# Two last steps of a token-mixing kernel change places, and the new last step gives its results in halves

## The chip, the cores and the metric

The kernel runs on one core of one Trainium2 chip. The metric is device time in microseconds, lower is better.

## What is computed

The input x has 8 batches of 4224 tokens and 192 channels. The first part of the reference is a causal 7-tap convolution along the tokens with softmax weights per head. On its result the second part mixes tokens with two 4224 x 4224 matrices, and then channels:

```python
theta = x @ w_theta
zr, zi = x * cos(theta), x * sin(theta)
y = einsum('ts,bsd->btd', w_tok_r, zr) + einsum('ts,bsd->btd', w_tok_i, zi)
u = x + y
out = u + maximum(u @ w_ch, 0)
```

Nearly all the work is in the two token products: for each of the 33 blocks of 128 output tokens, a sum over all 4224 input tokens, with 8 x 192 = 1536 columns. A 128 x 1536 result is called a row block here.

## The kernel before

**Chunks and steps.** The input tokens are cut into 33 chunks of 128. Eleven chunks are kept on the chip at a time, each as a tile `z` with seven fp16 planes: four products of x with cosine and sine, and sums and differences of them. The row blocks are taken in pairs, 17 units in all; the last unit has one block (32), since 33 is odd. The kernel goes round the units in 58 steps, t = 0 to 57. A step takes one unit and all chunks that are on the chip, multiplies them, adds the products to the unit's row block tiles `pv`, and writes these to scratch memory for the unit's next turn. A row block is finished at its unit's last turn. Towards the end fewer chunks are left for a step: step 55 has 6, step 56 (blocks 30 and 31) has 4, step 57 (block 32 alone) has 2.

**What a step does.** `load_w` (L316) fetches the two matrices' pieces into `st` by DMAs on POOL's queue, four for each matrix; there are two `st` buffers, one for each matrix, so the next step's load waits until the last transpose of the buffer. `turn` (L334) transposes a piece in 32 x 32 blocks on VectorE into a weight tile `wt`; `wsum` (L342) makes sums and differences of weight tiles, also on VectorE. For a pair of blocks, seven products per chunk do the work of eight: four transposes and four sums (S1 to S4) prepare the weights. For a single block there are two transposes, no sum, and four products. `mix` (L430) issues the products: for each entry of the list that `runs` (L410) returns, all the step's chunks in turn, two matmuls of 384 columns each (q = 0 and 1, the two halves of the columns), which accumulate in a PSUM tile `y` of two banks. Two such tiles exist. At the end of an entry, `give` (L400) has VectorE add the accumulator to one half (h) of the channels of a row block; the accumulator may go on after that.

**The end of a row block.** `cast` (L460) makes fp16 of half the row block (column group g, 768 columns), on ScalarE, or on VectorE for g = 0 in the last two steps. `turn_u` (L467) transposes it by six PE transposes (L165) into a PSUM tile `tp`, which ScalarE evacuates to `uT` (L151). `output` (L473) multiplies by `w_ch` in eight matmuls (L141) into a PSUM tile `v`; then one VectorE instruction (L476) adds the positive part to the row block, and one DMA on SP's queue (L481) writes 384 KB to the output. `tp` and `v` take turns in two PSUM buffers.

**Order.** The order on each engine is written down by hand: `pe`, `dve`, `act` and `pool` chain an engine's instructions in the order in which they are called. Within a step, `mix` calls events between products. An event's place is a number from 0 to 7, the share of the step in sevenths. The next step's transposes and sums are events of the current step (`w_tasks`, L354, called in `step_events`), and so are its loads of row blocks (`load_rows`, L365, on SP's queue), the weight loads of the step after it, and the casts, transposes and outputs of finished blocks (`outputs`, L486), which are placed by an estimate of the products' time, 0.324 us for each pair of matmuls.

Of the kernel before, what the change touches and what calls it, by code (L numbers as in the profile page):

```python
# [16 lines left out]
def kernel(  # L17
# [23 lines left out]
    nc = tc.nc  # L41
# [42 lines left out]
    def pe(ins):  # L84
        return in_order("pe", ins)

    def dve(ins):
        return in_order("dve", ins)
# [64 lines left out]
    def turned():  # L153
        return wk.tile([P, 12, P], F16, name="uT", tag="uT")
# [5 lines left out]
    def transposed(uT, u, gs, by_dve=False):  # L160

        tp = banks("tp", F16)
        for g in gs:
            for k in range(6):
                pe(nc.tensor.transpose(  # L165
                    tp[:, g, k * P : (k + 1) * P],
                    u[:, g * GC + k * P : g * GC + (k + 1) * P], ident,
                ))
        g = slice(gs[0], gs[-1] + 1)
        evacuate(  # L170
            uT[:, :, :].rearrange("p (g k) s -> p g (k s)", g=NG)[:, g, :],
            tp[:, g, 0 : 6 * P], by_dve,
        )
# [111 lines left out]
    class Step:  # L285


        def __init__(self, t):
            self.t, self.u, self.ks = t, unit(t), active(t)
            self.n = len(self.ks)  # L290
            self.tbs = [tb for tb in (2 * self.u, 2 * self.u + 1) if tb < NT]
            self.pair = len(self.tbs) == 2
            self.first = t < NU
            self.final = t + NU >= NSTEP
            self.late = self.final and self.n < NW
            visits = [v for v in range(NU, NSTEP) if v % NU == t % NU]
            quiet = [v for v in visits if start[2 * NW - 1] < v <= 2 * NU]
            self.adds, self.ahead = [], []
            for i, tb in enumerate(self.tbs):
                known = self.known(tb)  # L300
                if t not in ([v for v in quiet if known < v - 1] or visits[-1:])[:1]:
                    continue
                if not self.late:
                    self.adds.append(i)
                else:
                    far = known <= start[2 * NW - 1]
                    self.ahead.append((i, 2 * NU - NW + 2 * (t % NU) if far else start[-1],
                                       (t // NU - 1 - far) % 2))
            self.time = 0.324 * self.n * (7 if self.pair else 4)
            self.st, self.w, self.xr, self.ub, self.uT, self.pv = {}, {}, {}, {}, {}, []  # L310

        def known(self, tb):
# [41 lines left out]
        def w_tasks(self):  # L354

            if not self.pair:
                return [(0.25, lambda: self.turn("11")), (4.2, lambda: self.turn("12"))]
            return [
                (0.25, lambda: self.turn("11")), (1.2, lambda: self.turn("21")),
                (2.05, lambda: self.wsum("S3")), (2.2, lambda: self.turn("22")),  # L360
                (3.05, lambda: self.wsum("S1")), (3.3, lambda: self.wsum("S2")),
                (4.2, lambda: self.turn("12")), (5.1, lambda: self.wsum("S4")),
            ]
# [33 lines left out]
                    accum_op=ALU.add,  # L397
                ))

        def give(self, y, i, h, copies):  # L400
            o = self.pv[i][:, :].rearrange(
                "p (q b h e) -> p q b h e", q=2, h=2, e=HD
            )[:, :, :, h, :]
            yv = y[:, :, 0:BH].rearrange("p q (b e) -> p q b e", e=HD)
            if self.first and copies:
                act(nc.scalar.activation(out=o, in_=yv, func=AT.Copy))  # L406
            else:
                dve(nc.vector.tensor_tensor(out=o, in0=yv, in1=o, op=ALU.add))  # L408

        def runs(self):  # L410


            if self.pair:
                return [
                    ("11", Z11, "c1", True, (0, 0, True)),
                    ("S1", T1, "c2", True, (1, 1, True)),
                    ("S2", T2, "c1", False, (0, 1, True)),
                    ("S4", Z22, "c2", False, (0, 1, False)),
                    ("S3", T3, "c1", False, (1, 1, False)),
                    ("12", Z21, "c3", True, (0, 0, False)),  # L420
                    ("22", T4, "c1", False, (1, 0, True)),
                ]
            return [
                ("11", Z11, "c1", True, (0, 1, True)),
                ("11", T1, "c2", True, None),
                ("12", Z21, "c1", False, (0, 0, True)),
                ("12", Z22, "c2", False, (0, 1, False)),
            ]

        def mix(self, events):  # L430

            runs = self.runs()
            events = sorted(events, key=lambda e: e[0])
            y = {}
            for r, (wn, zn, cn, opens, to) in enumerate(runs):
                if opens:
                    y[cn] = ypool.tile([P, 2, PC], F32, name="y", tag="y")
                for c, k in enumerate(self.ks):
                    while events and events[0][0] * len(runs) <= 7 * (r + c / self.n):
                        events.pop(0)[1]()  # L440
                    yield k
                    for q in range(2):
                        pe(nc.tensor.matmul(  # L443
                            y[cn][:, q, 0:BH],
                            lhsT=self.w[wn][:, c, :, :].rearrange("p bt i -> p (bt i)"),
                            rhs=chunks[k].z[:, zn, q * BH : (q + 1) * BH],
                            start=(opens and c == 0), stop=(c == self.n - 1),
                            skip_group_check=True,
                        ))
                if to:  # L450
                    self.give(y[cn], *to)
            for _, f in events:
                f()
            if not self.final:
                for i, tb in enumerate(self.tbs):
                    nc.sync.dma_start(
                        out=part[(self.t // NU) % 2][tb, :, :], in_=self.pv[i]
                    )

        def cast(self, i, g):  # L460
            if g == 0:
                self.ub[i] = wk.tile([P, N], F16, name="ub", tag="ub", bufs=2)
                self.uT[i] = turned()
            cols = slice(g * GC, (g + 1) * GC)
            evacuate(self.ub[i][:, cols], self.pv[i][:, cols], self.t >= NSTEP - 2 and g == 0)

        def turn_u(self, i, g):  # L467
            transposed(self.uT[i], self.ub[i], [g])

        def cross_u(self, i):  # L470
            crossed(self.uT[i], self.ub[i])

        def output(self, i, g):  # L473
            u = self.pv[i][:, g * GC : (g + 1) * GC]
            ub = u.rearrange("p (k n) -> p k n", k=2)
            dve(nc.vector.scalar_tensor_tensor(  # L476
                out=ub, in0=channel_mix(self.uT[i][:, 6 * g : 6 * g + 6, :], wch), scalar=0.0, in1=ub,
                op0=ALU.max, op1=ALU.add,
            ))
            rows = slice(self.tbs[i] * P, (self.tbs[i] + 1) * P)  # L480
            nc.sync.dma_start(  # L481
                out=out[g * GB : (g + 1) * GB, rows, :].rearrange("b s d -> s b d"),
                in_=u.rearrange("p (b d) -> p b d", d=D),
            )

        def outputs(self):  # L486

            found = []
            for i in range(len(self.tbs)):
                if not self.late:  # L490
                    at = 1 if i or not self.pair else 0.9 - self.time / 7
                    for g in range(NG):
                        found.append((at + g, lambda i=i, g=g: self.cast(i, g)))
                        found.append((12 + 5.5 * i + 2.7 * g,
                                      lambda i=i, g=g: self.output(i, g)))
                    found.append((at + 2, lambda i=i: self.cross_u(i)))
                    continue
                at = 1.2 if i or not self.pair else 0.6 - self.time / 7
                every, turn, mix = 2.0, 1.2, 3.6
                for g in range(NG):  # L500
                    found.append((at, lambda i=i, g=g: self.cast(i, g)))
                    found.append((at + turn, lambda i=i, g=g: self.turn_u(i, g)))
                    found.append((at + mix, lambda i=i, g=g: self.output(i, g)))
                    at += every
            return found

    steps = [Step(t) for t in range(NSTEP)]
    outputs = [
        (sum(s.time for s in steps[: t + 1]) + at, f)
        for t in range(NSTEP) if steps[t].final for at, f in steps[t].outputs()  # L510
# [233 lines left out]
```

## Time and profile before

| | |
|---|---|
| median of three runs | 1448.68 us (1447.93 to 1449.42) |
| span of the profiled execution, first to last instruction | 1444.6 us |
| mean granted clock of TensorE | 0.997 |
| PE busy | 1414.5 us, 98% of the span |
| VectorE (DVE) busy | 978.2 us, 68% |
| ScalarE (ACT) busy | 316.2 us, 22% |
| start of the last product of L443 | 1429.4 us |
| end of the last instruction of VectorE | 1440.2 us |

The page gives the profiled execution by its span; a time of its own is not listed for it, and the median of the runs lies 4.1 us above the span. In rows of the order in time, the columns are the start, the duration (both us), the engine, the line, the operation, the tiles written and read with their shapes, the number of merged instructions, and in brackets the idle time before it and who ended it. PE's rows for matmuls include some 0.16 us of pipeline after the last issue, so that neighbouring rows overlap. In the table by stretches the numbers after the window are its length, then the busy time and count of PE, PEld (weight loads), DVE, ACT and POOL, the granted clock, the share of the DMA engines and GB/s.

### The profile page before, as it was taken

Reading aid. Unit: us, or ns where it says so; the run is one execution under the profiler, and the core shown is the slowest. Engines: PE = TensorE matmul, PEld = TensorE weight load, DVE = VectorE, ACT = ScalarE, POOL = GpSimd, SP = SyncE. Lnnn points to the kernel's source line nnn. Section 1 sums busy time; section 2 is a strip of 40 time slices with the busy share of each in tenths; the row PEclk is TensorE's granted clock in tenths of the full one; section 3 lists DMA queues with packets and bytes.
Section 4 is the critical chain, followed back from the end, with each engine's and each line's share of the span. In section 5 each row is a group of like instructions: output and inputs, shape, how many; then the busy total and the mean of one; then the engine's idle time right before and its main releaser. Section 6 shows DMA issues by size and latency. Waiting matters only on the chain.

```text
span 1444.6 us, 23749 instructions
## 1 busy us (share of the span) xinstructions
PE 1414.5 (98%) x9809; PEld 886.3 (61%) x9809; DVE 978.2 (68%) x1050; ACT 316.2 (22%) x379; POOL 434.6 (30%) x655
## 2 busy tenths in 40 slices
PE   7899999999999999999999999999999999999997
PEld 4656666666666666666666666666666666666665
DVE  6893554555448687866666657876877677767686
ACT  6851101111124254000000004435210110010133
POOL 8421211111223232432433343233323123213120
PEclk9999999999999999999999999999999999999999
DMA  9975756564699999897899889989999999898883
GB/s 181 253 148 136 146 119 133 98 152 87 152 229 210 226 244 222 219 265 173 223 245 222 233 155 239 235 181 237 274 220 202 213 204 221 204 200 193 166 232 116
DMA packets 272029, 281.99 MB, mean 195 GB/s; under 512 B 106672, under 2 KB 240176, under 8 KB 271920
## 3 DMA queue, kind: packets, MB, share of 16 engines
q0 software_dynamic: 162464, 92.15, 48.4%
q1 hardware_dynamic: 71824, 178.88, 35.2%
q10 hardware_dynamic: 37632, 9.44, 4.3%
q8 instruction: 77, 1.26, 0.4%
q14 instruction: 32, 0.26, 0.1%
HBM read 245.49 MB, written 108.13 MB: 245 GB/s over the span
## 4 chain that ended last, share of the span: by engine, by line
PE 89%; DVE 3%; DMA 2%; ACT 2%; POOL 1%; issue 1%; SPq 0%; DVEq 0%; ACTq 0%; POOLq 0%
PE y L443 81%; PE v L141 5%; PE pc L210 1%; PE tp L165 1%; ACT z L246 1%; DVE pv L408 1%; DMA xw<-xw 1%; POOL xw L197 1%; DMA xw<-in_x_dram 1%; DVE z L257 1%; POOL st L323 1%; DVE z L251 1%; DMA pv<-part 1%; ACT uT L151 1%; DVE wt L336 0%
## 5 line engine op out<-in xcount | busy, mean ns | idle before, releaser
L443 PE MATMUL y<-z,wt 128*128 128x384 f16 x7656 | 1283.6, 326 | 10.4 <-DVE pv L408 7.3
L443 PEld LDWEIGHTS <-wt 128*128 128x128 f16 x7656 | 740.7, 98 | 488.1 <-issue 10.2
L408 DVE TENSOR_TENSOR pv<-y,pv 128x768 f32<-128x768 f32 x324 | 309.2, 955 | 327.0 <-PE y L443 286.8
L336 DVE STREAM_TRANSPOSE wt<-st 128x1408 f16<-128x1408 f16 (+7 forms) x224 | 327.8, 1465 | 45.8 <-PE y L443 39.1
L323 POOL DMA_DIRECT2D st<-in_moe_w_tok_r_dram x232 | 132.4, 579 | 464.9 <-DVE wt L336 459.4
L323 POOL DMA_DIRECT2D st<-in_moe_w_tok_i_dram x232 | 132.5, 580 | 405.4 <-DVE wt L336 397.5
L348 DVE TENSOR_TENSOR wt<-wt 128x1408 f16<-128x1408 f16 (+7 forms) x216 | 176.1, 815 | 40.5 <-PE y L443 38.0
L151 ACT ACTIVATE z<-pc 128x768 f16<-128x768 f32 x65 | 53.3, 820 | 386.7 <-PE pc L210 386.5
L151 ACT ACTIVATE ub<-pv 128x768 f16<-128x768 f32 x63 | 50.2, 835 | 333.2 <-DVE pv L408 310.7
L406 ACT ACTIVATE pv<-y 128x768 f32<-128x768 f32 x66 | 54.0, 819 | 281.6 <-PE y L443 281.6
L141 PEld LDWEIGHTS <-uT 128*128 128x128 f16 x1056 | 91.1, 98 | 27.4 <-issue 8.5
L386 POOL TENSOR_TENSOR pv<-pv,xr 128x1536 f32<-128x1536 f32 x24 | 74.5, 3105 | 67.1 <-DVE pv L476 21.9
L197 POOL DMA_DIRECT2D xw<-in_x_dram x132 | 76.5, 591 | 30.1 <-DMA xw<-xw 9.7
L476 DVE SCALAR_TENSOR_TENSOR pv<-v,pv 128x768 f32<-128x768 f32 x66 | 62.9, 954 | 27.5 <-PE v L141 27.0
L151 ACT ACTIVATE uT<-tp 128x1536 f16<-128x1536 f16 (+1 forms) x49 | 59.7, 1221 | 74.4 <-PE tp L165 74.4
L257 DVE TENSOR_TENSOR z<-z 128x768 f16<-128x768 f16 x132 | 73.4, 556 | 3.6
L246 ACT ACTIVATE z<-v,half_pi 128x768 f16<-128x768 f32 x66 | 59.9, 907 | 42.1 <-PE v L141 41.7
L251 DVE TENSOR_TENSOR z<-z 128x1536 f16<-128x1536 f16 x66 | 60.1, 948 | 6.6 <-ACT z L246 6.6
L141 PE MATMUL v<-wth,uT 128*128 128x192 f16 x528 | 55.0, 248 | 5.6 <-ACT z L246 3.3
L141 PE MATMUL v<-wch,uT 128*128 128x192 f16 x528 | 54.2, 246 | 2.1 <-DVE pv L476 1.2
L246 ACT ACTIVATE z<-v 128x768 f16<-128x768 f32 x66 | 53.5, 810 | 0.0
L210 PE MATMUL pc<-xw,bands 96*64 96x192 f16 x528 | 35.3, 256 | 1.2 <-DVE bands L628 0.8
(43 smaller groups left out, 138.0 us busy)
## 6 DMA issues: line engine op xcount, KB each, us to landing
part<-pv SPq DMA_DIRECT2D x79, 768.0 KB, 4.6
pv<-part SPq DMA_DIRECT2D x79, 768.0 KB, 6.0
out_dram<-pv SPq DMA_DIRECT2D x66, 384.0 KB, 4.3
st<-in_moe_w_tok_r_dram POOLq DMA_DIRECT2D x136, 176.0 KB, 5.7
st<-in_moe_w_tok_i_dram POOLq DMA_DIRECT2D x136, 176.0 KB, 5.1
xs<-z SPq DMA_DIRECT2D x132, 96.0 KB, 4.1
xw<-in_x_dram POOLq DMA_DIRECT2D x121, 96.0 KB, 5.9
xr<-xs SPq DMA_DIRECT2D x24, 384.0 KB, 4.5
```

The costliest lines, as they stand in the source:

```text
L141: pe(nc.tensor.matmul(v[:, k, b * D : (b + 1) * D], lhsT=tT[:, 3 * k + b + i, :], rhs=w[:, 2 * b + i, :], start=(i == 0), stop=(i == 1),))
L151: act(nc.scalar.activation(out=out, in_=in_, func=AT.Copy))
L197: nc.gpsimd.dma_start(out=self.xw[lo : lo + n, h, :, :], in_=x[:, t0 : t0 + n, :].rearrange("b s d -> s b d"),)
L246: act(nc.scalar.activation(**args))
L251: dve(nc.vector.tensor_tensor(out=o, in0=xv, in1=o, op=ALU.mult))
L257: dve(nc.vector.tensor_tensor(out=z[:, o, :], in0=z[:, a, :], in1=z[:, b, :], op=ALU.subtract))
L323: pool(nc.gpsimd.dma_start(out=st[a * Q : (a + 1) * Q, 0:nb, :, 0:n] .rearrange("i r bt s -> i (r bt) s"), in_=w[self.tbs[0] * P : (self.t ...
L336: dve(nc.vector.transpose(self.w[name][:, 0 : self.n, :, :], self.st[int(name[1])][:, int(name[0]) - 1, :, 0 : self.n * Q] .rearrange("p b ...
L348: dve(nc.vector.tensor_tensor(out=self.w[name][:, 0 : self.n, :, :], in0=self.w[a][:, 0 : self.n, :, :], in1=self.w[b][:, 0 : self.n, :, : ...
L386: ins = pool(nc.gpsimd.tensor_tensor(out=self.pv[i], in0=self.pv[i], in1=self.xr[i], op=ALU.add))
L408: dve(nc.vector.tensor_tensor(out=o, in0=yv, in1=o, op=ALU.add))
L443: pe(nc.tensor.matmul(y[cn][:, q, 0:BH], lhsT=self.w[wn][:, c, :, :].rearrange("p bt i -> p (bt i)"), rhs=chunks[k].z[:, zn, q * BH : (q + ...
```

## The change

The list of steps ends with 57 and 56 instead of 56 and 57: block 32 alone (2 chunks) comes before the pair 30 and 31 (4 chunks), which is now the last step and is marked `closing`. For the closing step:

- the transposes and sums of its weights come in another order (12, 11, 21, 22, S1, S2, S4, S3), all of them as events of the one-block step;
- its seven products come in another order, in which the first row block (30) has its last addition after the fifth, and the second block (31) after the seventh;
- the last two products run as two column halves each: first q = 0 for all chunks and its addition, then q = 1 and its addition. `give` gets the half as a slice;
- block 30 is cast and put out as before, at other places; block 31 is cast by halves of the channels (`cast_half`): the half h = 1 at once on ScalarE, the half h = 0 in two column groups on VectorE;
- the eviction of block 31's second transpose is on VectorE, and the last output is written in two VectorE instructions and two DMAs of 192 KB.

The number of matmuls stays the same, 9809. VectorE gets five instructions more, ScalarE one less, SP's queue one DMA more.

```diff
@@ def w_tasks(self):
+            if self.closing:
+                return [
+                    (0.25, lambda: self.turn("12")), (0.6, lambda: self.turn("11")),
+                    (1.2, lambda: self.turn("21")), (2.2, lambda: self.turn("22")),
+                    (3.0, lambda: self.wsum("S1")), (3.6, lambda: self.wsum("S2")),
+                    (4.4, lambda: self.wsum("S4")), (5.1, lambda: self.wsum("S3")),
+                ]
...
-        def give(self, y, i, h, copies):
+        def give(self, y, i, h, copies, qs=slice(0, 2)):
             o = self.pv[i][:, :].rearrange(
                 "p (q b h e) -> p q b h e", q=2, h=2, e=HD
-            )[:, :, :, h, :]
-            yv = y[:, :, 0:BH].rearrange("p q (b e) -> p q b e", e=HD)
+            )[:, qs, :, h, :]
+            yv = y[:, qs, 0:BH].rearrange("p q (b e) -> p q b e", e=HD)
...
@@ def runs(self):
+            if self.closing:
+                return [
+                    ("12", Z21, "c2", True, (0, 0, False)),
+                    ("11", Z11, "c1", True, (0, 0, False)),
+                    ("S1", T1, "c3", True, (1, 1, False)),
+                    ("S2", T2, "c1", False, (0, 1, False)),
+                    ("S4", Z22, "c3", False, (0, 1, False)),
+                    ("S3", T3, "c1", False, (1, 1, False)),
+                    ("22", T4, "c1", False, (1, 0, False)),
+                ]
...
+        def products(self):
+            for r, (wn, zn, cn, opens, to) in enumerate(self.runs()):
+                last = self.n - 1
+                if not self.closing or r < 5:
+                    for c in range(self.n):
+                        yield (wn, zn, cn, c, opens and c == 0, c == last, (0, 1),
+                               to if c == last else None)
+                    continue
+                for q in range(2):
+                    for c in range(self.n):
+                        yield (wn, zn, cn, c, False, c == last, (q,),
+                               to + (slice(q, q + 1),) if c == last else None)
...
+        def cast_half(self, i, h, gs, by_dve):
...
+            bs = slice(gs.start * GB, gs.stop * GB)
+            o, u = (
+                v[:, :].rearrange("p (b h e) -> p b h e", h=2, e=HD)[:, bs, h, :]
+                for v in (self.ub[i], self.pv[i])
+            )
+            evacuate(o, u, by_dve)
...
-        def output(self, i, g):
+        def output(self, i, g, parts=1):
...
+            for j in range(parts):
+                ks = slice(2 * j // parts, 2 * (j + 1) // parts)
+                dve(nc.vector.scalar_tensor_tensor(
+                    out=ub[:, ks, :], in0=v[:, ks, :], scalar=0.0, in1=ub[:, ks, :],
+                    op0=ALU.max, op1=ALU.add,
+                ))
...
@@ def outputs(self):
+            if self.closing:
+                for g in range(NG):
+                    found.append((-2.5 + 0.1 * g, lambda g=g: self.cast(0, g)))
+                    found.append((-1.2 + 0.3 * g, lambda g=g: self.turn_u(0, g)))
+                    found.append((-0.5 + 0.4 * g, lambda g=g: self.output(0, g)))
+                found.append((-0.6, lambda: self.cast_half(1, 1, slice(0, NG), False)))
+                for g in range(NG):
+                    found.append((-0.55 if g == 0 else 0.01, lambda g=g: self.cast_half(
+                        1, 0, slice(g, g + 1), True)))
+                    found.append((0.02 + 0.1 * g, lambda g=g: self.turn_u(1, g, g == 1)))
+                    found.append((0.3 + 0.1 * g, lambda g=g: self.output(1, g, 1 + g)))
+                return found
...
-    steps = [Step(t) for t in range(NSTEP)]
+    order = list(range(NSTEP - 2)) + [NSTEP - 1, NSTEP - 2]
+    steps = [Step(t) for t in order]
+    steps[-1].closing = True
```

More of the change, by code (lines that the diff above doesn't have):

```diff
@@ L309, in __init__ @@
             self.time = 0.324 * self.n * (7 if self.pair else 4)
+            self.closing = False
             self.st, self.w, self.xr, self.ub, self.uT, self.pv = {}, {}, {}, {}, {}, []
@@ L430, in mix @@
         def mix(self, events):
-            runs = self.runs()
+            items = list(self.products())
+            total = sum(len(e[6]) for e in items)
             events = sorted(events, key=lambda e: e[0])
             y = {}
-            for r, (wn, zn, cn, opens, to) in enumerate(runs):
+            done = 0
+            for wn, zn, cn, c, opens, closes, qs, to in items:
                 if opens:
                     y[cn] = ypool.tile([P, 2, PC], F32, name="y", tag="y")
[L438 to L449, printed above, removed]
+                while events and events[0][0] * total <= 7 * done:
+                    events.pop(0)[1]()
+                k = self.ks[c]
+                yield k
+                for q in qs:
+                    pe(nc.tensor.matmul(
+                        y[cn][:, q, 0:BH],
+                        lhsT=self.w[wn][:, c, :, :].rearrange("p bt i -> p (bt i)"),
+                        rhs=chunks[k].z[:, zn, q * BH : (q + 1) * BH],
+                        start=opens, stop=closes,
+                        skip_group_check=True,
+                    ))
+                done += len(qs)
@@ L458, in mix @@
                     )
+        def cast_half(self, i, h, gs, by_dve):
+            if i not in self.ub:
+                self.ub[i] = wk.tile([P, N], F16, name="ub", tag="ub", bufs=2)
+                self.uT[i] = turned()
+            bs = slice(gs.start * GB, gs.stop * GB)
[4 more added lines that the diff above has]
+            evacuate(o, u, by_dve)
         def cast(self, i, g):
@@ L465, in cast, with turn_u @@
             evacuate(self.ub[i][:, cols], self.pv[i][:, cols], self.t >= NSTEP - 2 and g == 0)
-        def turn_u(self, i, g):
-            transposed(self.uT[i], self.ub[i], [g])
+        def turn_u(self, i, g, by_dve=False):
+            transposed(self.uT[i], self.ub[i], [g], by_dve)
         def cross_u(self, i):
             crossed(self.uT[i], self.ub[i])
-        def output(self, i, g):
+        def output(self, i, g, parts=1):
             u = self.pv[i][:, g * GC : (g + 1) * GC]
             ub = u.rearrange("p (k n) -> p k n", k=2)
[L476 to L479, printed above, removed]
+            v = channel_mix(self.uT[i][:, 6 * g : 6 * g + 6, :], wch)
@@ L480, in output @@
             rows = slice(self.tbs[i] * P, (self.tbs[i] + 1) * P)
[L481 to L484, printed above, removed]
+            for j in range(parts):
[3 more added lines that the diff above has]
+                    op0=ALU.max, op1=ALU.add,
+                ))
+                b0, nb = g * GB + GB * j // parts, GB // parts
+                nc.sync.dma_start(
+                    out=out[b0 : b0 + nb, rows, :].rearrange("b s d -> s b d"),
+                    in_=u.rearrange("p (b d) -> p b d", d=D)[
+                        :, GB * j // parts : GB * j // parts + nb, :
+                    ],
+                )
```

## The prediction

> **What bounds the kernel now.** I read the page first, then the table by stretches, the order in time of VectorE, ScalarE, PE and the queues for the last 50 us, and the chain that ended last.
>
> ```profile
> span 1444.6 us, 23749 instructions
> PE 1414.5 (98%) x9809; PEld 886.3 (61%) x9809; DVE 978.2 (68%) x1050; ACT 316.2 (22%) x379; POOL 434.6 (30%) x655
> ...
> 1394.00:1412.10 18.10, 17.66 (x140) 11.92 (x138) 14.70 (x21) 5.61 (x9) 4.34 (x8) 1.00 0.81 205
> 1412.10:1440.20 28.10, 23.23 (x206) 16.43 (x203) 20.65 (x26) 12.27 (x16) 0.00 (x0) 1.00 0.34 113
> ```
>
> PE is the bound for the whole (98%), but not at the end: in the last 28 us PE has 4.9 us without work and VectorE (DVE, fifth number) 7.5. The order of instructions of the changed program equals the old one on every engine up to the first weight transpose at 1394.45, so the change lives in what follows. There, the lines that I take prices from:
>
> ```profile
> 1406.19 0.70 DVE L336 STREAM_TRANSPOSE wt<-st 128x512 f16<-128x512 f16 x1
> 1407.18 2.17 POOL L323 DMA_DIRECT2D st<-in_moe_w_tok_i_dram  x4 [6.41 <-DVE wt L336]
> 1408.14 0.42 DVE L348 TENSOR_TENSOR wt<-wt 128x512 f16<-128x512 f16 x1
> 1411.16 0.96 DVE L408 TENSOR_TENSOR pv<-y,pv 128x768 f32<-128x768 f32 x1 [0.99 <-PE y L443]
> 1412.04 0.44 DVE L336 STREAM_TRANSPOSE wt<-st 128x256 f16<-128x256 f16 x1
> 1418.77 0.96 DVE L476 SCALAR_TENSOR_TENSOR pv<-v,pv 128x768 f32<-128x768 f32 x1 [0.60 <-PE v L141]
> 1420.70 0.96 DVE L476 SCALAR_TENSOR_TENSOR pv<-v,pv 128x768 f32<-128x768 f32 x1 [0.98 <-PE v L141]
> 1425.73 0.56 DVE L149 CAST ub<-pv 128x768 f16<-128x768 f32 x1
> 1429.37 0.83 PE L165 MATMUL tp<-ident,ub 128*128 128x128 f16 x12
> 1437.48 1.52 PE L141 MATMUL v<-wch,uT 128*128 128x192 f16 x16 [0.21 <-DVE pv L476]
> 1438.34 1.82 DVE L476 SCALAR_TENSOR_TENSOR pv<-v,pv 128x768 f32<-128x768 f32 x2 [0.91 <-PE v L141]
> ```
>
> A move or an output costs 0.96 us, or 0.87 when the next is ready (two take 1.82). 1418.77 to 1420.70 is one hop "output frees a PSUM buffer, eight products fill it, next output": 1.93 us. Eight products of L141 occupy PE for 0.66, six transposes of L165 for 0.33, a product of L443 for 0.16; all are readable some 0.2 us after that. The final stretch is such a chain:
>
> ```profile
> 1433.55 0.96 DVE pv L476
> 1434.53 0.97 DVE pv L476
> 1435.50 0.04 issue
> 1435.54 0.83 PE v L141 x8
> ...
> 1436.47 0.97 DVE pv L476
> ```
>
> In the old kernel the last product starts at 1429.37, and 10.8 us of casts, transposes, channel products and outputs follow, to 1440.16. Then the last output DMA (issue 1440.19, landed 1442.85) and the end at 1444.6. The median of the three runs, 1448.68, is 4.1 us above this span; I add differences of the span to it.
>
> **The change part by part.** Total work hardly changes: the same 72 products, ten groups of transposes and ten of channel products. What changes is what VectorE does when.
>
> *Swap.* The two-block step needs four transposes (0.70) and four sums (0.42), the one-block step two transposes of half the width (0.44). Formerly the eight stood inside the step before (1394 to 1409), where PE was busy 17.66 of 18.10 us: they cost nothing there, and taking them away gains nothing there, since the PE waits of that stretch (0.1 and 0.3 us) end on outputs and casts that stay. Now they stand in the one-block step, which has only 2.6 us of products, behind the move at 1411.16.
>
> *Queues that the step is moved past.* On POOL the wide loads trade places with the narrow ones: the i load (four of 64 KB) still waits for the narrow transpose that replaces the one at 1406.19, so it is issued from 1407.0 to 1409.2. The narrow loads there (16 KB) landed 1.9 to 2.7 us after issue; 64 KB ones issued at 1388 under load took 5.8 to 5.9. That gives 1410.7 to 1414.5; I take 1412.1, because the DMA engines have no other work after 1410. Cost then 0.1, and up to 2.3. On SP the row loads of the new last step take the places of the old ones; the last is issued near 1403.8 (landing 1408.6 in the old trace) and needed at 1425: hidden with 16 us to spare.
>
> *Stage A, VectorE's queue.* In the new order, after 1412.1: four transposes, four sums, three moves of the one-block step, one output, the first move of the last step, one cast. Transposes 4 x 0.66 = 2.6, sums 4 x 0.40 = 1.6, five of about 0.89 = 4.5, cast 0.56: 9.3, with small gaps 1421.6. PE waits three times here: its third group of products needs the first move, which is queued behind two transposes (1.8 us), and it cannot open two later accumulators before moves that stand behind the sums (0.4 and 1.2).
>
> *Stage B, hops.* An output at 1421.7 frees the buffer for the next eight products: one hop, 1423.6; a move to 1425.5; two products and eight channel products, 1.25 to the output at 1426.8; hop, 1428.6; move, done 1430.5. The first row block's last move follows at 1431.5, so it does end early; its outputs do not, as they stand behind the second block's moves.
>
> *Stage C, the halves.* The last two products are split into column halves, but in the program's order PE's first product of every half waits for VectorE's move of the half before, even where the columns differ. So they do not overlap. A half move: 0.70 against 0.44 for transposes of 512 and 256 columns gives 0.17 fixed; so 0.17 + 0.79/2 = 0.56. Products with the channel products placed among them: 1432.0; VectorE first finishes a move, a cast and an output (1432.9), half move to 1433.5. Second half: 0.05 + 0.65 + 0.2 and 0.56, 1434.95. Third, with twelve transposes among the products: 1.6 and 0.56, 1437.1. Fourth, with eight channel products: products done 1438.65, but an output goes first, so moved at 1439.6; output of the first block to 1440.5; half cast 0.35, 1440.8; six transposes, 1441.35; eviction by VectorE 0.56 (bounds 0.56, the cast of the same width, and 0.96), 1441.9; eight products, 1442.8; output of the first column group until 1443.0, two half outputs 0.47 + 0.56: 1444.0. Against 1440.16: **+3.85**. The same working, done for the old order with the same prices, ends at 1440.15.
>
> *Last DMA.* 384 KB at the 371 to 379 GB/s that the DMA view shows here is 1.05 us, half of that 0.5: **-0.5** (bounds -0.6 and 0).
>
> *Clock.* Near the start the trace has two stretches at half clock (0.50 in the ninth number), each behind one in which PE was busy less than half:
>
> ```profile
> 5.45:8.87 3.42, 1.57 (x32) 1.59 (x32) 1.62 (x8) 1.37 (x2) 3.42 (x8) 1.00 1.53 202
> 8.87:12.28 3.41, 3.38 (x27) 2.36 (x28) 1.46 (x3) 0.81 (x1) 3.36 (x6) 0.50 1.48 171
> 32.76:36.17 3.41, 1.67 (x14) 0.59 (x12) 3.27 (x6) 2.29 (x3) 2.41 (x5) 1.00 1.16 194
> 36.17:39.59 3.42, 3.15 (x20) 2.12 (x20) 3.39 (x7) 1.02 (x2) 1.24 (x3) 0.50 1.35 239
> ```
>
> The old tail stays above that (its emptiest stretch of that length has PE busy for 2.08 of 3.41 us). In my table PE has 1.4 us between 1432.2 and 1435.6, less than 1.57, so the products from 1435.6 on may run at half clock. Twice the PE time of the third and fourth half comes to 1.7 at most; where the windows lie differently it is 0. I take **+0.8**. The Trainium skill ("TensorE: Matmul & The Clock Gate", "Why this matters for your kernels") asks only that PE have no gap above about 3 us between bursts, since one idle window brings the half clock. By that rule the term would be 0 and the sum 0.8 lower, as my longest gap is 1.7; the rows above, with PE 46 and 49% busy, say that less than idleness is enough.
>
> Sum: +3.85 - 0.5 + 0.8 = **+4.2**, span 1448.8, time **1452.9** (+0.29%).
>
> **The rivals.** *PE does not wait for the other half* (the split works as the change says). For it: the columns differ. Against: the waits stand in the program. Without them stage C ends 2.1 earlier: 1441.9, with the shorter DMA +1.2, time **1449.9**. Decided by whether PE's idle time ahead of the second half is zero.
>
> *Faster: VectorE never waits.* The change makes 5.4 of the 10.8 us behind the last product disappear, and if VectorE ran its new list without a gap, 23.6 us (17 at 0.87, six halves at 0.47, transposes 2.5, sums 1.5, copies 2.0), it would end at 1435.7: -4.5, with the DMA **1443.7**. It decides if fewer than 1.4 of the 8.3 us of idle time in my table are real. Against it: the hops of L476 and L141 stay serial, and the old tail, in the row above, had 7.5 us of such idle time.
>
> *The wide i load lands late*: every microsecond behind 1412.1 moves all that follows; at 1414.5 and half clock the sum is 2.3 + 0.9 higher, **1456.1**.
>
> **How the numbers follow.** Forecast with its small errors (half clock or not) 0.70; halves free 0.13; late load 0.10; VectorE without gaps 0.07. Range 1449.9 to 1456.0: from the second case to the late load, which leaves out the faster one and half of the late load's tail. A measurement can tell about 0.2%, 2.9 us, from no change. Slower by more: forecast (less 0.05 for its lower edge) and late load, 0.75; within: 0.18; faster: 0.07.
>
> **What would show it.** Right: VectorE without gaps above 0.2 us from 1412 to 1421, PE idle about 1.7 us ahead of its third group in the one-block step and again ahead of the second half, last L476 ending near 1444 to 1446, one half-clock window near 1436. Wrong: the transposes and sums hidden before 1412; a half starting while the other's move runs; an end of L476 before 1441.

## The result and the profile after

| | before | after |
|---|---|---|
| median of the first comparison | 1448.40 us (9 runs) | 1453.56 us (9 runs) |
| ratio, 95% interval | | 1.0028 [1.0017, 1.0039] |
| median of a second comparison | 1448.63 us (35 runs) | 1451.15 us (11 runs) |
| ratio, 95% interval | | 1.0014 [0.9999, 1.003] |
| profiled execution: time, span | -, 1444.6 us | 1453.77 us, 1452.0 us |

The change makes the kernel slower: by 0.28% in the first comparison, where the forecast was 0.29%, and by 0.14% in the second, whose interval just includes no change. The page of the changed kernel shows the same work, PE still at 98%:

```profile
span 1452.0 us, 23759 instructions
PE 1416.2 (98%) x9809; PEld 887.6 (61%) x9809; DVE 976.7 (67%) x1055; ACT 315.5 (22%) x378; POOL 433.9 (30%) x655
```

Spans are 7.4 us apart, but 4.0 of that lies ahead of the change: the first weight transpose of the third-last step, up to which both kernels have the same instructions in the same order (two weight loads shortly ahead of it, which already belong to the exchanged steps, are narrower), starts at 1394.45 before and at 1398.47 after. So I count a **tail** from the start of that transpose to the end of VectorE's last instruction. Two profiles of each kernel give 45.71 and 45.73 us before, 49.25 and 49.09 after: **+3.45** on the mean. The start of the tail was somewhere else in every profile: 1394.45 and 1396.56 before, 1398.47 and 1396.09 after. In the table by stretches (length, then busy time and count of PE, PEld, DVE, ACT, POOL, granted clock, DMA share, GB/s) PE's work differs from before only in the second row, the last two steps and what follows:

```profile
1398.00:1416.10 18.10, 17.65 (x140) 11.92 (x138) 11.55 (x14) 5.59 (x9) 4.56 (x8) 1.00 0.90 205
1416.10:1447.72 31.62, 23.19 (x206) 16.35 (x203) 24.68 (x37) 11.65 (x15) 0.00 (x0) 1.00 0.30 101
```

VectorE has 3 us less to do in the first row and 4 more in the second; PE does its 23.2 us in 31.6 instead of 28.1. VectorE's order in time for stage A:

```profile
1398.47 0.43 DVE L337 STREAM_TRANSPOSE wt<-st 128x256 f16<-128x256 f16 x1
...
1416.42 1.30 DVE L337 STREAM_TRANSPOSE wt<-st 128x512 f16<-128x512 f16 x2 [0.29 <-DMA st<-in_moe_w_tok_i_dram]
1417.65 0.92 DVE L416 TENSOR_TENSOR pv<-y,pv 128x768 f32<-128x768 f32 x1
...
1425.53 0.96 DVE L527 SCALAR_TENSOR_TENSOR pv<-v,pv 128x768 f32<-128x768 f32 x1 [0.23 <-PE v L141]
```

The first transpose of the closing step waits 0.29 us for the i load (the load of `w_tok_i`); then VectorE has no gap until 1425.30. The move at 1417.65 stands behind two transposes, and PE waits for it, as the first of these rows of PE shows:

```profile
1418.62 0.81 PE L477 MATMUL y<-z,wt 128*128 128x384 f16 x4 [1.35 <-DVE pv L416]
1424.02 0.81 PE L477 MATMUL y<-z,wt 128*128 128x384 f16 x4 [0.94 <-DVE pv L416]
...
1437.33 0.81 PE L477 MATMUL y<-z,wt 128*128 128x384 f16 x4 [1.52 <-DVE pv L416]
1438.79 0.32 PE L477 MATMUL y<-z,wt 128*128 128x384 f16 x1 [0.65 <-DVE pv L416]
...
1440.92 0.32 PE L477 MATMUL y<-z,wt 128*128 128x384 f16 x1 [0.65 <-DVE pv L416]
```

The last three are the second half of the sixth product and the two halves of the seventh: each waits for VectorE's move of the half before. VectorE's own rows there:

```profile
1438.18 0.56 DVE L416 TENSOR_TENSOR pv<-y,pv 128x384 f32<-128x384 f32 x1 [0.90 <-PE y L477]
1440.31 0.56 DVE L416 TENSOR_TENSOR pv<-y,pv 128x384 f32<-128x384 f32 x1 [1.57 <-PE y L477]
...
1445.83 1.89 DVE L527 SCALAR_TENSOR_TENSOR pv<-v,pv 128x768 f32<-128x768 f32 x3 [0.17 <-PE v L141]
```

The two engines take turns. The last output ends at 1447.72.

### The profile page after: what moved, and what is told of

It is laid out like the page before. It is cut to its first block, busy times and chain, and to the rows that moved or that the text cites. A ratio compares the mean times of both kernels' runs of the same rounds, so it can differ in the third digit from the quotient of the medians.

```text
span 1452.0 us, 23759 instructions
## 1 busy us (share of the span) xinstructions
PE 1416.2 (98%) x9809; PEld 887.6 (61%) x9809; DVE 976.7 (67%) x1055; ACT 315.5 (22%) x378; POOL 433.9 (30%) x655
## 3 DMA queue, kind: packets, MB, share of 16 engines
q8 instruction: 77, 1.26, 0.4%
## 4 chain that ended last, share of the span: by engine, by line
PE 85%; DVE 6%; DMA 5%; issue 2%; ACT 1%; POOL 1%; DVEq 0%; SPq 0%; POOLq 0%; ACTq 0%
PE y L477 77%; PE v L141 5%; DMA st<-in_moe_w_tok_i_dram 2%; PE pc L210 1%; PE tp L165 1%; DVE z L257 1%; DVE z L251 1%; DVE pv L416 1%; DVE wt L337 1%; DVE wt L349 1%; DMA st<-in_moe_w_tok_r_dram 1%; DMA xw<-xw 1%; DVE pv L527 1%; ACT z L246 1%; DMA part<-pv 1%
## 5 line engine op out<-in xcount | busy, mean ns | idle before, releaser
L416 DVE TENSOR_TENSOR pv<-y,pv 128x768 f32<-128x768 f32 (+1 forms) x326 | 309.4, 949 | 327.9 <-PE y L477 288.6
L527 DVE SCALAR_TENSOR_TENSOR pv<-v,pv 128x768 f32<-128x768 f32 (+1 forms) x67 | 63.0, 942 | 26.4 <-PE v L141 26.1
L246 ACT ACTIVATE z<-v,half_pi 128x768 f16<-128x768 f32 x66 | 59.8, 906 | 41.6 <-PE v L141 41.3
```

Of the source, the lines that this page charges most:

```text
L246: act(nc.scalar.activation(**args))
L527: dve(nc.vector.scalar_tensor_tensor(out=ub[:, ks, :], in0=v[:, ks, :], scalar=0.0, in1=ub[:, ks, :], op0=ALU.max, op1=ALU.add,))
```

## The experiments

All tails are counted as above. To the left of each tail stand its two parts: when the last product of a token mix (one matmul of 384 columns) starts, counted from the start of the tail, and how far behind that start VectorE's last instruction ends. The last product before starts at 1429.21; the 1429.37 of the forecast is the start of the transposes behind it, so that 10.95 stands here for the forecast's 10.8. Ratios are against the kernel before, with the 95% interval.

| kernel | last product at | behind it | tail | ratio |
|---|---|---|---|---|
| before, twice | 34.8 | 10.95 | 45.71, 45.73 | |
| after, twice | 43.6, 43.4 | 5.65 | 49.25, 49.09 | 1.0028, 1.0014 |
| exchange alone | 38.7 | 9.2 | 47.97 | 1.0018 [1.0007, 1.003] |
| exchange, weights a step earlier | 36.7 | 9.2 | 45.94 | 0.9999 [0.999, 1.0007] |
| the same, end ordered anew | 37.9 | 7.2 | 45.11 | 0.9993 [0.9983, 1.0002] |
| after, weights a step earlier, twice | 42.6 | 5.65 | 48.25, 48.25 (half clock) | 1.0005 [0.9997, 1.0014] |
| after, whole moves, cast too early | 41.5 | 6.2 | 47.70 | 1.001 [1.0001, 1.0019] |
| after, whole moves, cast behind | 41.5 | 8.35 | 49.84 (half clock) | 1.0029 [1.002, 1.0039] |
| after, one move for both halves, cast too early | 41.6 | 6.05 | 47.69 | 1.001 [1.0001, 1.0019] |
| weights earlier, whole moves, cast too early | 39.6 | 6.2 | 45.85 | 1.0003 [0.9994, 1.0012] |
| closing treatment, no exchange | 42.1 | 8.8 | 50.91 (half clock; the count begins late, see below) | 1.0052 [1.0039, 1.0065] |

In the three kernels marked "cast too early", the fp16 copy of 384 columns of block 31 is taken before the last product is added: the `cast_half` that stands behind the first half move in the changed kernel keeps its place, while the move comes later. Their times are read with that; the row "cast behind" mends it.

**The changed kernel again.** Theory: the tail costs what it costs, the rest is chance ahead of it.

> The changed kernel once more. The tail is counted from the first weight transpose of the third-last step to the end of VectorE's last instruction: 45.71 us before, 49.24 after, +3.53. The rest of the difference of the medians (5.2) is put to chance in what lies ahead of that transpose, where both kernels are the same instruction for instruction. If so, the tail is 49.2 again within 0.3, the point at which it begins lies anywhere from 1394 to 1399, and the median comes to 3 to 5.5 us above the kernel before. The rival, that the change also costs time ahead of the tail, wants that point near 1398.5 again. A half clock in the tail (term +0.8 of the sum) would show as a window at 0.50 behind 1430 and a tail of 50.

The tail is 49.09 and begins at 1396.09, 2.4 us earlier than in the first profile; the median is 2.5 us above the kernel before, a little under what was expected. So the 5.2 us between the medians of the first comparison is not all the tail's. No half clock in the tail.

Where the 4.0 us ahead of the tail come from can be read in the first profile of each kernel. The first transpose of 128x1408 starts at 106.00 before and at 107.95 after: 1.95 are there already. Another 1.91 are one wait of PE in the middle, on a move that stands behind a transpose for which VectorE waited 4.7 us for an i load:

```profile
634.96 6.33 PE L477 MATMUL y<-z,wt 128*128 128x384 f16 x38 [1.91 <-DVE pv L416]
```

The second profile of the changed kernel has the same wait with 0.91 us, and of the other twelve only one has such a wait (0.67, whole moves), though the instructions there are the same in all. Whether the changed kernel is prone to it or this is chance, two profiles don't tell.

**The kernel before again.**

> The kernel before, for one more look. All differences of tails rest on its 45.71 us; two profiles of the changed kernel differ by 0.16 and two of the kernel with early weights by less than 0.01, so 45.7 within 0.2 is expected again, wherever the tail begins.

45.73, starting at 1396.56. The profile on which the forecast was built was thus one that came to the tail 2 us early, and its tail was as always. This run's time, 1448.79, is 2.1 above its span of 1446.7.

**The exchange alone.** `steps[-1].closing = True` is left out.

```diff
     order = list(range(NSTEP - 2)) + [NSTEP - 1, NSTEP - 2]
     steps = [Step(t) for t in order]
-    steps[-1].closing = True
```

> The two last steps change places, and nothing else: the last step's products, moves, casts and outputs keep their old form. If the exchange is what costs (weights of the pair prepared behind the products that hide them, then the chain of outputs and channel products), the tail is 48.2 to 48.6 us, +2.5 to +2.9 over before, and the time 2.5 to 3 us over before. If the closing step's halves and its own order cost the time (rival), the tail is 45.7 to 46.5 and the time that of before.

The tail is 47.97, 2.25 longer than before, a little below what was expected. The exchange makes some two thirds of the loss, the closing step's form the other 1.2.

**The exchange with the weights a step earlier.** The loads and weight tiles of the last step go to buffers of finished chunks, and its transposes and sums to the step before the one-block step.

```diff
+            if self.early:
+                st = zpool.tile([P, 2, NQ, n], F16, name="stc", tag="z")
...
-            found += steps[t + 1].w_tasks()
+            if not steps[t + 1].early:
+                found += steps[t + 1].w_tasks()
+            if t + 2 < NSTEP and steps[t + 2].early:
+                found += [(0.3 + a, f) for a, f in steps[t + 2].w_tasks()]
...
+        if t + 3 < NSTEP and steps[t + 3].early:
+            for m in (1, 2):
+                found.append((0.5, lambda m=m: steps[t + 3].load_w(m)))
...
```

> The two last steps change places, everything else of the last step is in the old form, and its transposes and sums are done a step earlier, as before the change. Beside the kernel with the exchange alone (tail 47.97) only the weights differ. If VectorE's queue of weights in the one-block step is the whole price of the exchange, the tail is that of the kernel before, 45.3 to 46.1 us, and the time within 1 us of it. If the chain of outputs and channel products of three row blocks costs as well, it stays above 46.5.

45.94, 0.2 above before: the queue of weights is 2.03 of the 2.25 us that the exchange costs. PE's order in time shows where. The exchange alone:

```profile
1415.32 0.81 PE L477 MATMUL y<-z,wt 128*128 128x384 f16 x4 [0.40 <-DVE pv L416]
...
1419.41 1.46 PE L477 MATMUL y<-z,wt 128*128 128x384 f16 x8 [1.29 <-DVE pv L416]
1421.47 0.81 PE L477 MATMUL y<-z,wt 128*128 128x384 f16 x4 [0.60 <-DVE pv L416]
```

and with the weights earlier, for the same groups:

```profile
1414.49 0.81 PE L487 MATMUL y<-z,wt 128*128 128x384 f16 x4 [0.40 <-DVE pv L426]
...
1417.12 2.30 PE L487 MATMUL y<-z,wtc 128*128 128x384 f16 x12
```

The waits of 1.29 and 0.60 are gone (the second and third rows are one run of twelve), and with them nearly all of the 2.03.

**The same with the end ordered anew.** Casts of block 30 on both engines and its transposes go beside the last product; block 31's casts stand ahead of the outputs, one eviction is on VectorE, the last output is in two parts.

```diff
+            if self.early:
+                return [
+                    (-1.0, lambda: self.cast_by(0, 0, True)),
+                    (-0.95, lambda: self.cast_by(0, 1, False)),
+                    (-0.6, lambda: self.turn_u(0, 0, False)),
+                    (-0.2, lambda: self.turn_u(0, 1, False)),
+                    (0.001, lambda: self.cast_by(1, 0, True)),
...
```

> The same with the end of the last step ordered anew: both groups of block 30 are cast and transposed while the last product runs, the casts of block 31 stand ahead of all outputs, one of its evictions is on VectorE, and its last output comes in two parts. Summed up by row prices, it ends 0.9 us earlier than with the old order at the end: tail 44.5 to 45.2, below that of the kernel before (45.7); in the time that is 0.5 to 1 us, less than the runs can tell.

45.11, 0.6 below the kernel before, and its emptiest stretch of 3.41 us has 2.26 us of PE. Its ratio, 0.9993 with 1 inside the interval, shows no gain that a measurement could tell.

**The changed kernel with the weights a step earlier.** The edit is the one above, on the changed kernel.

> The changed kernel with the last step's four transposes and four sums done one step earlier, inside the six-chunk step, where PE has 13 us of products to hide them (their loads come a step earlier too, into buffers that finished chunks have left). Nothing else moves. If stage A, VectorE's queue in the one-block step, is what the exchange costs, the tail falls from 49.2 to 46.6 to 46.9 us, 2.4 to 2.6 less, and PE's idle time of 1.35 and 0.94 us ahead of the one-block step's third group and the next accumulator goes to 0.5 or less. If the tail is set by the hops of channel products and outputs alone (rival), PE only reaches them earlier and waits there: less than 0.5 us is gained.

Only 0.9 less, 48.25. Yet the first half move starts 36.0 us into the tail, 2.2 earlier than after, and the waits of 1.35 and 0.94 are down to 0.40 and none: stage A's price was paid back. It is lost behind the first half move, and the table by stretches (ninth number: granted clock) shows how. The kernel with early weights:

```profile
1429.25:1432.66 3.41, 1.24 (x9) 0.61 (x8) 2.16 (x4) 0.61 (x1) 0.00 (x0) 1.00 0.34 115
1432.66:1436.07 3.41, 2.76 (x19) 1.86 (x17) 0.92 (x2) 2.32 (x3) 0.00 (x0) 0.50 0.00 0
```

and the changed kernel at the same place of its tail:

```profile
1434.92:1438.33 3.41, 1.71 (x13) 0.99 (x12) 2.47 (x5) 0.84 (x1) 0.00 (x0) 1.00 0.35 118
1438.33:1441.75 3.42, 2.31 (x26) 1.82 (x26) 1.32 (x3) 2.21 (x3) 0.00 (x0) 1.00 0.17 56
```

PE was busy for 1.24 us of one stretch and got half the clock in the next; with 1.71 us it did not. From the first half move to the end it is 10.98 us in both profiles of the changed kernel, 12.24 here: +1.26. A second profile of the same kernel:

> The kernel with the weights a step earlier once more, for one look. Its first profile has a stretch at half clock from 1432.66 to 1436.06, behind 3.41 us in which PE was busy for 1.25, and a tail of 48.25 us; its first half move starts 36.0 us into the tail (38.3 in the changed kernel). If the half clock cost it the 1.3 us by which its last stretch is longer than that of the changed kernel, and came by the chance of where the stretches of 3.41 us lie, then a profile without it has a tail of 46.9 to 47.2; one with it has 48.2 again. If the last stretch is longer for another reason (rival), the tail is 48.2 at full clock too.

It had the half clock again, from 1434.66, and the tail is 48.25 again; 12.22 from the first half move to the end. What the half clock costs is so told only by the comparison with the changed kernel (+1.25, and 1.23 of it between the second and the third half move), not by a profile of this kernel without it. In the runs this kernel is 0.7 us slower than before (interval -0.4 to 2.0), less than the 2.5 of its tails; how many of these runs had the half clock is not on record.

**Whole moves, and one move for both halves.** In `products` the split at `r < 5` becomes `r < 7` (whole moves); or the order by halves stays and `give` comes once, for both column halves:

```diff
-                               to + (slice(q, q + 1),) if c == last else None)
+                               to + (slice(0, 2),) if c == last and q else None)
```

> The changed kernel with the last two products in one piece: four half moves (0.55 each) become two whole ones (0.96 each), and PE waits at one place in place of three. If the halves serialise, as stage C has it, they cost time: the tail gets 1.1 us shorter, 48.0 to 48.3. If they overlap as intended, the tail gets longer, by up to 2 us: 50 to 51.

> The last two products keep their order by column halves, but VectorE moves the whole row block half once, after both column halves. If it is the two extra waits and moves of the halves that cost, and not the order of the products, the tail is that of the kernel with whole moves, 47.5 to 47.9 us. If the order of products costs (rival), it stays near 49.

47.70 and 47.69, some 1.5 less than after, as if the serial halves cost that. But both take the cast of 384 columns too early. With `cast_half` moved behind the last addition:

```diff
-                    found.append((-0.55 if g == 0 else 0.01, lambda g=g: self.cast_half(
+                    found.append((0.005 if g == 0 else 0.01, lambda g=g: self.cast_half(
```

> Whole moves for the last two products again, with block 31's first VectorE cast placed behind its last addition. In the kernels with whole moves before this one that cast stayed where the first half move had made it possible, and so took its 384 columns without the last product: its 0.35 us and what waits for it lay too early. If that is what made them 1.5 us shorter than the changed kernel, the tail is 48.7 to 49.2 now, and the halves neither gain nor lose. If the serial waits are what the halves cost (stage C), it stays near 47.7 to 48.1.

49.84, above what was expected, with a half clock at its end:

```profile
1437.40:1440.81 3.41, 1.34 (x15) 0.98 (x12) 3.02 (x5) 0.90 (x2) 0.00 (x0) 1.00 0.34 114
1440.81:1444.22 3.41, 3.01 (x22) 2.70 (x23) 0.77 (x3) 0.81 (x1) 0.00 (x0) 0.50 0.37 120
```

Six transposes (0.33) and eight products (0.66) of its last chain lie in that row, so at full clock it would be about 1.0 shorter, 48.8, an estimate. By this estimate the halves neither gain nor lose much: the table has the last product 2.0 us later with them, and less to do behind it, since the first 384 columns are cast (at 1440.90) before the last half move (1442.81).

**Weights earlier and whole moves.**

> The weights a step earlier and the last two products in one piece, the two edits together. If their gains add up, the tail is 45.3 to 45.8 us, that of the kernel before (45.7), the time within 1 us of it, and PE has no stretch of 3.41 us with less than 1.7 us of work, so no half clock. If one edit uses up the other's gain, the tail stays at 46.5 or more.

45.85, and no half clock: the gains of the two edits add up, 1.85 for the weights (47.70 to 45.85). The early cast is in both kernels.

**The closing treatment without the exchange.** `order = list(range(NSTEP))`, and `steps[-2].closing = True`.

> The other part of the change alone: the pair's step keeps its old place (its weights are prepared in the step before, where products hide them), but takes the closing step's order of sums, products, halves, casts and outputs; the one-block step is last, in its old form. The pair gains from hidden weights and loses by its serial halves, and behind them come the one-block step's own products, two casts and its chain of outputs. By the row prices the tail is 51 us, 5.3 longer than before, time 1453 to 1454. If the closing treatment does end the pair early (rival), the tail is 45 or less.

50.91 by this count, near the 51 that was expected, but not by the sum that was expected. The closing order begins with the transpose `12`, which reads the i matrix; here it is the first of the third-last step, and it waits for that load:

```profile
1390.74 0.97 DVE L337 STREAM_TRANSPOSE wt<-st 128x768 f16<-128x768 f16 x1
...
1400.09 1.30 DVE L337 STREAM_TRANSPOSE wt<-st 128x512 f16<-128x512 f16 x2 [1.91 <-DMA st<-in_moe_w_tok_i_dram]
```

From the 128x768 transpose in the first row, the last weight transpose that all fourteen profiles share, to the start of the tail it is 9.35 us here and 7.36 in the thirteen others. Counted from there, VectorE ends 7.2 us later than before, not 5.2, and that fits the ratio (+7.5 us). The 7.2 hold the 2.0 of the late start, which the row prices left out, and a half clock from 1446.56 behind a stretch with 0.51 us of PE. The pair's step does not end early enough to pay for the one-block step behind it.

## Why the prediction came out right, point by point

*Swap and stage A: right.* VectorE had no gap but 0.29 us for 9.2 us (1416.14 to 1425.30; forecast 9.3, with 0.1 for the load), and PE waited 1.35, 0.21 and 0.94 (forecast 1.8, 0.4, 1.2). The experiments give this queue 2.0 us (47.97 to 45.94) and 1.85 (47.70 to 45.85). The i load landed 3.7 to 4.3 us after its issue, between the two bounds, and cost the 0.29: the rival of the late load falls.

*Stage B: right.* On the clock of the old profile (4.02 less) the outputs start at 1421.5, 1423.5, 1426.6 and 1428.5, forecast 1421.7, 1423.6, 1426.8 and 1428.6.

*Stage C: right in its place and size.* The half moves end at 1433.3, 1434.7, 1436.9 and 1439.3 on that clock (forecast 1433.5, 1434.95, 1437.1, 1439.6), the last output at 1443.7 (1444.0). The rival "PE does not wait for the other half" was to be decided by PE's idle time ahead of the second half: it is 1.52, not zero. A kernel whose halves are free of each other wasn't tried: the program's waits cover the whole accumulator tile. What the prediction did not ask was whether halves are worse than whole moves: by the estimate above they are not, by more than some tenths.

*"Faster: VectorE never waits": wrong, as weighed.* VectorE is busy for 35.8 us of the tail's 49.2, and for 34.9 of 45.7 before: its idle time grew by 2.7. The part of this rival that was true is in the table: what lies behind the last product shrank from 10.95 to 5.65. The last product moved back by 8.7.

*Last DMA: the term of -0.5 was mis-sized, it measures -0.06.* I priced the landing by size over bandwidth. The DMA view of the changed kernel, from 1440 on (KB each, median us to landing):

```profile
out_dram<-pv SPq DMA_DIRECT2D x3, 384.0 KB, 2.5
out_dram<-pv SPq DMA_DIRECT2D x2, 192.0 KB, 2.5
```

Half the bytes land as late as all; the last landing is 2.63 us behind VectorE's end, 2.69 before. The Trainium skill ("DMA: Bandwidth & Descriptors", "Anatomy of one DMA — SWDGE (gpsimd) path") states a fixed part of about 2.0 us for each DMA on another queue than this one. It points the same way. An estimate by that section's formula (bytes over 436 GB/s beside the fixed part) has half the bytes still save 0.45 us; here the row decides.

*Clock: the term of +0.8 was mis-sized, it measures 0 in both profiles of the changed kernel (no half clock near 1436) and, by comparison, 1.25 in its sister with early weights.* It behaves less like a size than like a chance: where the stretches of 3.41 us lie against PE's idle time. PE's rows in the changed kernel hold a stretch of that length with 1.24 us of work (1435.39 to 1438.80); the clock's own stretch began 0.5 us earlier and had 1.71. The page's rule that was weighed ("TensorE: Matmul & The Clock Gate", "Why this matters for your kernels") gave 0, and that held for this kernel; for its sister, whose longest PE gap was 1.5 us, it did not. The same page ("What's actually happening") calls the stretches free-running. The rows agree: in the sister's two profiles the half clock begins 2.3 and 2.0 us behind the first half move.

*Around the span: the 4.1 us were two things.* 2.1 lie around the span before (1448.79 against 1446.7), 1.8 after; the other 2.0 was a profile that was quick ahead of the tail. Why 0.3 less lies around the changed kernel's span isn't shown. With measured terms the sum is +3.45 - 0.06 - 0.3 = +3.1 us, inside the intervals of both comparisons (+4.1, from 2.5 to 5.6, and +2.0, from -0.1 to 4.3). The forecast's +4.2 came near it with two terms of the wrong size and opposite signs, and that it met the first comparison's +4.1 within 0.1 is luck. Why that comparison lies higher than the sum isn't shown; what lies ahead of the tail differs by as much between profiles.

## What to carry to other kernels

Before steps are exchanged, ask what each of them hid for its neighbour: a long step hides the next one's preparation, and a short one puts in its place brings that preparation onto the path; here doing it one step earlier gave back 2.0 of 2.25 us. Work split into halves gained nothing here, where each wait still covers the whole accumulator tile; whether it pays with waits by halves wasn't run. A shorter chain behind the last product gains nothing when the last product moves back by as much. Where a profile's span differs by several us between runs of one kernel, compare from the last instruction that both kernels share, and make sure that it is shared: in the kernel without the exchange the count began 2.0 us late.

## What was not expected of the hardware

- The half clock came behind stretches in which PE was busy for 1.24, 1.27 and 1.34 us of 3.41, though its longest gap was no more than 1.5 us in the kernel with early weights; a stretch with 1.71 was followed by full clock. No single limit on PE's busy time fits all: near the start of the changed kernel a stretch with 1.83 us was followed by half clock, and in the tail of the kernel without the exchange one with 1.59 by full clock:

```profile
35.47:38.88 3.41, 1.83 (x16) 0.85 (x16) 3.23 (x8) 1.56 (x3) 1.64 (x3) 1.00 1.09 156
38.88:42.29 3.41, 3.41 (x22) 2.05 (x20) 3.41 (x6) 2.13 (x3) 1.96 (x4) 0.50 1.34 260
...
1429.49:1432.91 3.42, 1.59 (x13) 1.01 (x13) 1.68 (x3) 0.15 (x2) 0.00 (x0) 1.00 0.34 115
1432.91:1436.32 3.41, 2.76 (x30) 2.24 (x28) 1.96 (x4) 2.21 (x3) 0.00 (x0) 1.00 0.00 0
```

- Output DMAs of 192 and 384 KB both landed 2.5 us after their issue.
- Thirteen profiles, all but that of the kernel without the exchange, reached the tail between 1394.3 and 1398.9 us, while tails of one kernel repeat within 0.2.
